# Attention tile ends: who copies four PSUM banks out, where that is emitted, and weight preparation with one more empty step

## The chip, the cores and the metric

The kernel runs on one core of a Trainium2 chip. The metric is device time in microseconds, the median of several runs. Five engines work side by side, each through its own queue in order: TensorE (PE, matmuls; its weight loads are PEld), VectorE (DVE), ScalarE (ACT), GpSimd (POOL) and SyncE (SP), which here only issues DMAs.

## The reference

Attention without softmax, gated by u, and then two feed-forward layers with the same sizes, all in float32:

```python
scores = (1.0 / S) * np.matmul(z, z.transpose(0, 2, 1))      # z: 2 x 3008 x 64
x = u * np.matmul(np.maximum(scores, 0.0) ** 2, v)           # u, v: 2 x 3008 x 256
h = x.reshape(6016, 256) @ w_in1                             # 256 x 2048
x = np.where(h > 0, h, np.exp(np.minimum(h, 0)) - 1) @ w_out1
h = x @ w_in2
out = ((a0 + a1*h + a2*h**2 + a3*h**3) / (1 + abs(b0)*abs(h) + abs(b1)*h**2 + 1e-6)) @ w_out2
```

## The kernel before

Every float32 operand of a matmul is split into a high part and the rest, and a product takes three matmuls: high by high, rest by high, high by rest. Tokens lie along the free axis, so the outputs are transposed (256 features in two halves of 128 partitions, `d` = 0 and 1).

**Attention.** There are 12 query tiles (`spans`, index `ti`): five of 512 tokens and one of 448 for each of two batches. Each is multiplied with 24 chunks of 128 keys (`j`; the last has 64). A step `n` is one tile and chunk, 288 in all (`NA`). At even `n`, `scores(n)` issues six matmuls (L283) for chunks `n` and `n+1` into one of two pairs of banks (0 and 1, or 2 and 3); ScalarE computes the relu (L286) and its square, which is the high part (L287); VectorE multiplies the scores by the relu, in PSUM (L289). At odd `n`, `scores_lo(n-1)` subtracts the high part from that product (L296), which gives the rest and frees the pair of banks. Four steps later (`LAG`), `values(n-4)` multiplies with v: 12 matmuls (L320), each on 64 of the 128 rows, so that two run side by side. They accumulate over the 24 chunks into banks 4 to 7. Key rows 0 to 63 (`h` = 0) and 64 to 127 (`h` = 1) have sums of their own, so `acc[ti][d, h]` are four banks: (1,0) is bank 4, (0,1) bank 5, (0,0) bank 6, (1,1) bank 7. A step's first six matmuls go to banks 4 and 5, the next six to 6 and 7.

**A tile's end** is the `values` of the last chunk, `j` = 23, at step 24 ti + 27. Only banks 6 and 7 still get six matmuls there. `out_of(ti, 1, w)` is emitted ahead of them and empties banks 4 and 5: VectorE multiplies bank 4 by u into `xo` (L339), ScalarE copies bank 5 into `t` (L340). `out_of(ti, 0, w)`, behind them, does the same with 6 and 7 (into `xo` and `e`). GpSimd then multiplies each copy by u (L328) and adds it to `xo` (L329); SP stores `xo` to DRAM (L330). For the last tile VectorE does what GpSimd does for the others. The next tile's first chunk needs banks 4 and 5 right after the six matmuls of the next `scores`.

**Side work.** `todo[n]` holds what else is emitted at step `n`. 32 blocks of the weight matrices arrive as 64-bit words and are turned into float32 pairs in stages: load (SP, L189), four steps later `size` (ScalarE, L197), then one step apart `words` (VectorE, L201 and L203), `powers` (VectorE, L208 and L210), `split` (ScalarE, L216 and L217) and `rest` (three operations on GpSimd, L221 to L228). 18 blocks stay in SBUF (the second batch's steps); 14 are stored to DRAM (L230, L231), during the first batch, and loaded again later. Among these are the loads and splits of v (L160; L169 on ScalarE, L170 on GpSimd), of z (L125; L137 and L138 on VectorE) and the loads of u (L270). Loads of weights, v and u share one tag, `raw`, with three buffers.

**Order.** `manual_schedule` keeps each engine's queue in the order in which the code emits. A step emits `scores` or `scores_lo`, then its `todo`, then `values`, and from step 288 on the steps of the feed-forward layers (`ffn_step`), which take the rest of the time.

Of the kernel before, what the change touches and what calls it, by code (L numbers as in the profile page):

```python
# [11 lines left out]
ALU = mybir.AluOpType  # L12
# [4 lines left out]
def f(ap):  # L17
    return ap.bitcast(F32)
# [3 lines left out]
def attention_then_two_ffns(  # L22
# [16 lines left out]
    nc = tc.nc  # L39
# [16 lines left out]
    for bb in range(B):  # L56
        i0 = 0
        while i0 < S:
            w = min(W, S - i0)
# [26 lines left out]
    def sb(tag, bufs, dt=F32, name=None):  # L86
        return sp.tile([P, W], dt, tag=tag, bufs=bufs, name=name or tag)

    def sb2(tag, bufs, dt=F32R):
        return sp.tile([P, 2, W], dt, tag=tag, bufs=bufs, name=tag)  # L90

    def wide(dt=F32R):
        return wp.tile([P, 2, W], dt, tag="w", name="w")
# [51 lines left out]
    def load_raw():  # L145
        return sp.tile([P, 2, 2 * P, 2], U32, tag="raw", bufs=3, name="raw")
# [31 lines left out]
    def stages_w(which, kind, g, keep):  # L178

        src = ((w_in1, w_out1), (w_in2, w_out2))[which][kind]
        c0 = 2 * g * P
        st = {}

        def load():
            part = src[:, c0:c0 + 2 * P] if kind == 0 else src[c0:c0 + 2 * P]
            raw = load_raw()
            nc.sync.dma_start(  # L189
                out=raw.rearrange("p k f t -> p k (f t)"),  # L190
                in_=part.bitcast(U32).rearrange("(k p) f -> p k f", p=P))
            raw = raw.rearrange("p k f t -> p (k f) t")
            st["lower"], st["upper"] = raw[:, :, 0], raw[:, :, 1]

        def size():
            st["y"] = sb("q", 3, U32)
            nc.scalar.activation(f(st["y"]), f(st["upper"]), AF.Abs)  # L197

        def words():
            y, u = st["y"], st["upper"]  # L200
            nc.vector.scalar_tensor_tensor(  # L201
                out=f(u), in0=f(y), scalar=LEAST, in1=f(u), op0=ALU.is_ge, op1=ALU.mult)
            nc.vector.tensor_scalar(  # L203
                out=y, in0=u, scalar1=3, scalar2=0x3FFFFFFF, op0=ALU.logical_shift_left, op1=ALU.bitwise_and)

        def powers():
            y, u = st["y"], st["upper"]
            nc.vector.scalar_tensor_tensor(  # L208
                out=y, in0=u, scalar=0xC0000000, in1=y, op0=ALU.bitwise_and, op1=ALU.bitwise_or)
            nc.vector.tensor_scalar(out=u, in0=y, scalar1=0xFF800000, scalar2=None, op0=ALU.bitwise_and)  # L210

        def split():
            if keep:
                st["t"] = wide()
            st["hi"] = st["t"][:, 0] if keep else sb("q", 3, F32R)
            nc.scalar.copy(st["hi"], f(st["y"]))  # L216
            nc.scalar.activation(f(st["lower"]), st["lower"], AF.Copy, scale=2.0**-52)  # L217

        def rest():
            hi, y, l = st["hi"], f(st["y"]), f(st["lower"])  # L220
            nc.gpsimd.tensor_tensor(out=y, in0=y, in1=f(hi), op=ALU.subtract)  # L221
            nc.gpsimd.tensor_tensor(out=l, in0=l, in1=f(st["upper"]), op=ALU.mult)
            if keep:
                lo = st["t"][:, 1]
                nc.gpsimd.tensor_tensor(out=lo, in0=y, in1=l, op=ALU.add)
                WS[kind][which, g] = [t.rearrange("p (k f) -> p k f", k=2) for t in (hi, lo)]
            else:
                nc.gpsimd.tensor_tensor(out=y, in0=y, in1=l, op=ALU.add)  # L228
                d = dp.tile([P, 2, W], F32, tag=f"wd{kind}{g}", name=f"wd{kind}{g}")
                nc.sync.dma_start(out=d[:, 0], in_=f(hi))  # L230
                nc.sync.dma_start(out=d[:, 1], in_=y)  # L231
                WD[which, kind, g] = d

        return load, size, words, powers, split, rest

    def stages_reload(which, kind, g):
        st = {}
# [21 lines left out]
    xd = {}  # L259
    hl = {}  # L260
    acc = {}

    us = {}
    LAG = 4
# [7 lines left out]
    def scores(n):  # L272

        ti, j = divmod(n, NCH)
        bb, i0, w = spans[ti]
        r, l = Z[bb, i0 // W]
        sr, sl = Z[bb, j // 4]
        i = n % 4
        s = psum[:, i:i + 2, :w]
        for k, (lhs, rhs) in enumerate(((sr, r), (sl, r), (sr, l))):  # L280
            for h in range(2):
                rows, c = slice(h * DQ, (h + 1) * DQ), (j + h) % 4 * P
                nc.tensor.matmul(s[:, h], lhsT=lhs[rows, c:c + P], rhs=rhs[rows, :w], start=k == 0, stop=k == 2)  # L283
        hi = sb2("hl", 3)
        e = wide(F32)[:, :, :w]
        nc.scalar.activation(e, s, AF.Relu, scale=SCALE)  # L286
        nc.scalar.activation(hi[:, :, :w], e, AF.Square)  # L287

        nc.vector.scalar_tensor_tensor(out=s, in0=s, scalar=SCALE, in1=e, op0=ALU.mult, op1=ALU.mult)  # L289
        hl[n] = hi  # L290

    def scores_lo(n):
        w = spans[n // NCH][2]
        hi, lo = hl.pop(n), sb2("x", 3)
        i = n % 4
        nc.vector.tensor_tensor(  # L296
            out=lo[:, :, :w], in0=psum[:, i:i + 2, :w], in1=f(hi[:, :, :w]), op=ALU.subtract)
        for h in range(2):
            hl[n + h] = hi[:, h], lo[:, h]
        if n >= NA - 4:  # L300
            free_banks.extend((i, i + 1))

    def values(n):
        ti, j = divmod(n, NCH)
        bb, i0, w = spans[ti]
        if j == 0:

            acc[ti] = {way: psum[:, 4 + k] for k, way in enumerate(((1, 0), (0, 1), (0, 0), (1, 1)))}
        hi, lo = hl.pop(n)
        vh, vl = V[bb, j // 2]  # L310
        if j == NCH - 1:
            xd[ti] = dp.tile([P, ND, W], F32, tag=f"xd{ti}", name=f"xd{ti}")
            out_of(ti, 1, w)


        for way in ((1, 0), (0, 1))[j == NCH - 1:]:
            for k, (lhs, rhs) in enumerate(((vh, hi), (vl, hi), (vh, lo))):
                for h, d in enumerate(way):
                    rows = slice(h * P // 2, (h + 1) * P // 2)
                    nc.tensor.matmul(  # L320
                        acc[ti][d, h][:, :w], lhsT=lhs[rows, j % 2, d * P:(d + 1) * P], rhs=rhs[rows, :w],
                        start=j == 0 and k == 0, stop=k == 2 and j == NCH - 1 - (h != d))
        if j == NCH - 1:
            x, y = out_of(ti, 0, w)

            eng = nc.gpsimd if ti < NTL - 1 else nc.vector
            for d in range(ND):
                eng.tensor_tensor(out=y[d], in0=y[d], in1=us[ti][:, d, :w], op=ALU.mult)  # L328
                eng.tensor_tensor(out=x[d], in0=x[d], in1=y[d], op=ALU.add)  # L329
                nc.sync.dma_start(out=xd[ti][:, d, :w], in_=x[d])  # L330
            del acc[ti], us[ti], sums[ti]

    sums = {}

    def out_of(ti, d, w):

        x, y = sums.setdefault(ti, ({}, {}))
        x[d], y[1 - d] = sb("xo", 2)[:, :w], (sb("t", 3) if d else sb("e", 3))[:, :w]
        nc.vector.tensor_tensor(out=x[d], in0=acc[ti][d, 0][:, :w], in1=us[ti][:, d, :w], op=ALU.mult)  # L339
        nc.scalar.copy(y[1 - d], acc[ti][1 - d, 1][:, :w])  # L340
        if ti == NTL - 1:
            free_banks.extend((4, 5) if d else (6, 7))
        return x, y


    a0, a1, a2, a3 = (coef[:, i:i + 1] for i in range(4))
# [18 lines left out]
    def split_x1(ti):  # L365
        w = ftiles[ti][1]
        raw = x1[ti][:, :, :w]
        hi, lo = ([t[:, d, :w] for d in range(ND)] for t in (sb2("rl", 2), sb2("rl", 2)))
        for d in range(ND):
            nc.vector.tensor_copy(hi[d], raw[:, d])  # L370
        for d, eng in enumerate((nc.vector, nc.gpsimd)):
            eng.tensor_tensor(out=lo[d], in0=raw[:, d], in1=f(hi[d]), op=ALU.subtract)
        x1[ti] = list(zip(hi, lo))
# [225 lines left out]
    n = 0  # L599
# [149 lines left out]
    NA = NTL * NCH  # L749
# [26 lines left out]
    for each, n0, n1 in ((halves, 26, HALF - 10), (direct, HALF + 4, NA - 16)):  # L776
        for k, key in enumerate(each):
            n = n0 + k * (n1 - n0) // len(each)
# [8 lines left out]
    for n in sorted(x for x in todo if x < 0):  # L787
        for fn in todo.pop(n):
            fn()
    for n in range(NA + NSTEP):  # L790
        if n < NA and n % 2 == 0:
            scores(n)
        if n < NA and n % 2:
            scores_lo(n - 1)
        for fn in todo.pop(n, ()):
            fn()
        if LAG <= n < NA + LAG:
            values(n - LAG)
        if n == NA - 3:
            split_x1(0)  # L800
        if n >= NA:
            ffn_step(n - NA)
# [30 lines left out]
```

## Time and profile before

| | |
|---|---|
| Time, median of 3 runs | 1642.83 us (1642.64 to 1643.84) |
| The profiled execution | 1645.2 us, of which the span is 1643.4 us |
| PE busy | 1574.1 us, 96% of the span |
| DVE busy | 1396.5 us, 85% |
| ACT busy | 1303.5 us, 79% |
| POOL busy | 746.3 us, 45% |
| Mean granted TensorE clock | 0.985 |

Busy shares are means over stages that differ. A row of the timeline has the start, the duration (of several instructions merged, from the first start to the last end), engine, line, operation and tiles, and in brackets how long the engine had been idle and whose work released it. PEclk is the granted TensorE clock as a share of full speed: 1.00 is 2.4 GHz and 0.50 is 1.2 GHz.

### The profile page before, as it was taken

The page shows a single profiled execution, that of the slowest core. Times are in us where ns is not written, and L with a number is a line of the kernel's source. Part 1 is how long each engine was busy: PE and PEld are TensorE (multiplying, and loading weights), DVE is VectorE, ACT ScalarE, POOL GpSimd, SP SyncE. Part 2 cuts the span into 40 slices and gives each one's busy share as a digit, 9 for nine tenths or more (in the row PEclk, how much of TensorE's full clock was granted, in tenths as well). Part 3 has the DMA queues.
Part 4 walks back from the last instruction along what each step waited for, and adds up shares of the span by engine and source line. Part 5 has one row for each costly group of instructions (what it writes and reads, how often), then busy time and mean ns, then how long its engine had stood idle before and what let it go on. Part 6 is the DMA issues. An engine that isn't in the chain of part 4 may idle for free.

```text
span 1643.4 us, 25037 instructions
## 1 busy us (share of the span) xinstructions
PE 1574.1 (96%) x9240; PEld 1324.9 (81%) x9240; DVE 1396.5 (85%) x1866; ACT 1303.5 (79%) x2035; POOL 746.3 (45%) x591
## 2 busy tenths in 40 slices
PE   8999998999989999999999999999999999998896
PEld 6877897888889888887878787878788787887796
DVE  7787888987877568889898989898888989899998
ACT  6666776776766688988888888889898888887786
POOL 3334443333433354444454444454444445447645
PEclk9999999999999999999999999999999999999999
DMA  4223343112221420000000000000000000000000
GB/s 126 74 92 115 104 134 110 63 59 78 65 65 60 151 66 0 24 1 27 1 1 27 1 26 1 26 1 27 1 27 1 1 20 1 21 0 13 1 14 14
DMA packets 40987, 67.15 MB, mean 41 GB/s; under 512 B 5536, under 2 KB 18336, under 8 KB 40864
## 3 DMA queue, kind: packets, MB, share of 16 engines
q1 hardware_dynamic: 40864, 65.55, 12.5%
q8 instruction: 72, 1.18, 0.3%
q14 instruction: 51, 0.42, 0.1%
HBM read 45.88 MB, written 19.66 MB: 40 GB/s over the span
## 4 chain that ended last, share of the span: by engine, by line
PE 63%; DVE 12%; ACT 5%; issue 3%; POOL 1%; POOLq 0%; DVEq 0%; ACTq 0%
PE psum L320 11%; PE psum L255 8%; PE psum L391 8%; PE psum L392 8%; PE psum L394 8%; PE psum L256 8%; PE psum L254 8%; PE psum L283 3%; DVE x L521 2%; DVE t L523 1%; DVE e L424 1%; DVE q L500 1%; DVE q L522 1%; DVE psum L289 1%; POOL hl L433 1%
## 5 line engine op out<-in xcount | busy, mean ns | idle before, releaser
L527 POOL TENSOR_TENSOR x<-t,r 128x512 fp32r<-128x512 f32 (+1 forms) x182 | 239.7, 1317 | 470.1 <-DVE t L523 455.1
L320 PE MATMUL psum<-hl,w 64*128 64x512 f32 (+1 forms) x2256 | 377.8, 398 | 29.0 <-DVE xo L339 28.0
L320 PEld LDWEIGHTS psum<-hl,w 64*128 64x128 f32 x2256 | 246.7, 190 | 62.2 <-ACT w L286 12.6
L433 POOL TENSOR_TENSOR hl<-e,hl 128x512 fp32r<-128x512 f32 (+1 forms) x192 | 246.2, 1282 | 31.3 <-ACT hl L432 30.2
L320 PE MATMUL psum<-x,w 64*128 64x512 f32 (+1 forms) x1128 | 247.4, 395 | 0.0
L286 ACT ACTIVATE w<-psum 128x1024 f32<-128x1024 f32 (+1 forms) x144 | 145.0, 1007 | 127.8 <-PE psum L283 126.4
L289 DVE SCALAR_TENSOR_TENSOR psum<-psum,w 128x1024 f32<-128x1024 f32 (+1 forms) x144 | 173.9, 1207 | 78.0 <-ACT w L286 77.7
L472 ACT ACTIVATE t<-psum,coef 128x512 f32<-128x512 f32 (+1 forms) x192 | 148.0, 771 | 82.6 <-PE psum L394 82.6
L498 DVE SCALAR_TENSOR_TENSOR q<-q,coef,psum 128x512 f32<-128x512 f32 (+1 forms) x166 | 122.0, 735 | 81.7 <-ACT q L491 81.6
L296 DVE TENSOR_TENSOR x<-psum,hl 128x1024 fp32r<-128x1024 f32 (+1 forms) x144 | 172.9, 1201 | 11.6 <-ACT q L197 0.5
L255 PE MATMUL psum<-hl,w 128*128 128x512 f32 (+2 forms) x416 | 157.4, 378 | 3.1 <-POOL hl L433 2.7
L391 PE MATMUL psum<-x,w 128*128 128x512 f32 (+2 forms) x416 | 154.2, 374 | 5.5 <-DVE t L523 5.5
L391 PE MATMUL psum<-rl,w 128*128 128x512 f32 (+2 forms) x416 | 154.3, 374 | 2.3 <-DVE e L424 1.6
L254 PE MATMUL psum<-hl,w 128*128 128x512 f32 (+2 forms) x416 | 155.8, 374 | 0.5 <-ACT hl L432 0.5
L256 PE MATMUL psum<-hl,w 128*128 128x512 f32 (+2 forms) x416 | 155.6, 374 | 0.0
L287 ACT ACTIVATE hl<-w 128x1024 fp32r<-128x1024 f32 (+1 forms) x144 | 150.5, 1045 | 4.6
L392 PE MATMUL psum<-rl,w 128*128 128x512 f32 (+2 forms) x416 | 153.9, 373 | 0.0
L392 PE MATMUL psum<-x,w 128*128 128x512 f32 (+2 forms) x416 | 153.8, 373 | 0.0
L255 PE MATMUL psum<-x,w 128*128 128x512 f32 (+2 forms) x384 | 147.2, 383 | 3.8 <-POOL x L527 3.7
L254 PE MATMUL psum<-x,w 128*128 128x512 f32 (+2 forms) x384 | 146.7, 382 | 3.1 <-DVE t L523 3.1
L424 DVE SCALAR_TENSOR_TENSOR e<-e,psum 128x512 f32<-128x512 f32 (+1 forms) x192 | 128.5, 669 | 22.3 <-ACT e L419 22.3
L256 PE MATMUL psum<-x,w 128*128 128x512 f32 (+2 forms) x384 | 146.6, 382 | 0.0
(150 smaller groups left out, 3657.5 us busy)
## 6 DMA issues: line engine op xcount, KB each, us to landing
raw<-w_in_dram SPq DMA_DIRECT2D x16, 512.0 KB, 4.1
raw<-w_out_dram SPq DMA_DIRECT2D x16, 512.0 KB, 4.1
wd<-q SPq DMA_DIRECT2D x28, 256.0 KB, 2.3
raw<-wd SPq DMA_DIRECT2D x14, 512.0 KB, 3.5
raw<-v_dram SPq DMA_DIRECT2D x22, 256.0 KB, 3.9
raw<-uT_dram SPq DMA_DIRECT2D x10, 512.0 KB, 4.3
xd<-xo SPq DMA_DIRECT2D x20, 256.0 KB, 2.1
outT_dram<-xo SPq DMA_DIRECT2D x20, 256.0 KB, 2.1
```

The source lines that it names most:

```text
L254: nc.tensor.matmul(out, lhsT=lh, rhs=rh, start=start, stop=False)
L255: nc.tensor.matmul(out, lhsT=lh, rhs=rl, start=False, stop=False)
L256: nc.tensor.matmul(out, lhsT=ll, rhs=rh, start=False, stop=stop)
L287: nc.scalar.activation(hi[:, :, :w], e, AF.Square)
L289: nc.vector.scalar_tensor_tensor(out=s, in0=s, scalar=SCALE, in1=e, op0=ALU.mult, op1=ALU.mult)
L296: nc.vector.tensor_tensor(out=lo[:, :, :w], in0=psum[:, i:i + 2, :w], in1=f(hi[:, :, :w]), op=ALU.subtract)
L320: nc.tensor.matmul(acc[ti][d, h][:, :w], lhsT=lhs[rows, j % 2, d * P:(d + 1) * P], rhs=rhs[rows, :w], start=j == 0 and k == 0, stop=k == 2 ...
L391: nc.tensor.matmul(h[:, cols], lhsT=wh[:, d, c], rhs=x[d][0], start=d == 0, stop=False)
L392: nc.tensor.matmul(h[:, cols], lhsT=wl[:, d, c], rhs=x[d][0], start=False, stop=False)
L433: nc.gpsimd.tensor_tensor(out=lo, in0=e, in1=f(hi), op=ALU.subtract)
L472: act(new("p", "t", 3), h, AF.Identity, bias=a2, scale=a3)
L527: tt(out=st["lo"], in0=st["p"], in1=st["r"], op=ALU.mult)
```

## The change

`out_of` copies both of its banks on ScalarE and no longer multiplies on VectorE. GpSimd (VectorE for the last tile) first adds the two halves of a sum and then multiplies by u, so there are four operations a tile on GpSimd as before. In the main loop `values` is emitted ahead of the step's `todo`; at step 4 alone it comes ahead of `scores` too. An empty stage stands between `powers` and `split`, so `split` and `rest` of every weight block come one step later.

```diff
-        return load, size, words, powers, split, rest
+        return load, size, words, powers, lambda: None, split, rest
...
         if j == NCH - 1:
-            x, y = out_of(ti, 0, w)
+            out_of(ti, 0, w)
 
             eng = nc.gpsimd if ti < NTL - 1 else nc.vector
             for d in range(ND):
-                eng.tensor_tensor(out=y[d], in0=y[d], in1=us[ti][:, d, :w], op=ALU.mult)
-                eng.tensor_tensor(out=x[d], in0=x[d], in1=y[d], op=ALU.add)
-                nc.sync.dma_start(out=xd[ti][:, d, :w], in_=x[d])
+                x, y = sums[ti][d, 0], sums[ti][d, 1]
+                eng.tensor_tensor(out=x, in0=x, in1=y, op=ALU.add)
+                eng.tensor_tensor(out=x, in0=x, in1=us[ti][:, d, :w], op=ALU.mult)
+                nc.sync.dma_start(out=xd[ti][:, d, :w], in_=x)
...
     def out_of(ti, d, w):
 
-        x, y = sums.setdefault(ti, ({}, {}))
-        x[d], y[1 - d] = sb("xo", 2)[:, :w], (sb("t", 3) if d else sb("e", 3))[:, :w]
-        nc.vector.tensor_tensor(out=x[d], in0=acc[ti][d, 0][:, :w], in1=us[ti][:, d, :w], op=ALU.mult)
-        nc.scalar.copy(y[1 - d], acc[ti][1 - d, 1][:, :w])
+        for k, c in enumerate((d, 1 - d)):
+            t = sums.setdefault(ti, {})[c, k] = (sb("xo", 2) if k == 0 else sb("t", 3) if d else sb("e", 3))[:, :w]
+            nc.scalar.copy(t, acc[ti][c, k][:, :w])
         if ti == NTL - 1:
             free_banks.extend((4, 5) if d else (6, 7))
-        return x, y
...
     for n in range(NA + NSTEP):
+
+        if n == LAG:
+            values(0)
         if n < NA and n % 2 == 0:
             scores(n)
         if n < NA and n % 2:
             scores_lo(n - 1)
+        if LAG < n < NA + LAG:
+            values(n - LAG)
         for fn in todo.pop(n, ()):
             fn()
-        if LAG <= n < NA + LAG:
-            values(n - LAG)
```

## Rows read from the trace of the kernel before

**Rows 1.** Windows: length; PE, PEld, DVE, ACT, POOL busy (count); PEclk, DMA share, GB/s.
```profile
0.00:552.00 552.00, 512.10 (x4282) 450.81 (x4283) 447.91 (x475) 377.61 (x445) 207.11 (x171) 0.97 0.28 88
552.00:1643.40 1091.40, 1061.96 (x4960) 874.08 (x4958) 948.57 (x1392) 925.86 (x1590) 539.16 (x420) 0.99 0.05 17
```
**Rows 2.** The waits of PE: total us, times, the longest.
```profile
PE psum L320 <- DVE xo L339: 28.0, 11, 4.5
...
PE psum L320 <- ACT t L340: 1.0, 1, 1.0
```
**Rows 3.** The timeline of PE and ACT at the first tile's end.
```profile
53.51 0.84 PE L283 MATMUL psum<-rl 64*128 64x512 f32 x6
55.98 0.72 PE L320 MATMUL psum<-hl,w 64*128 64x512 f32 x4 [1.63 <-DVE xo L339]
...
58.86 0.87 PE L283 MATMUL psum<-rl 64*128 64x512 f32 x6
...
62.34 0.87 PE L283 MATMUL psum<-rl,x 64*128 64x512 f32 x6
...
52.67 1.06 ACT L287 ACTIVATE hl<-w 128x1024 fp32r<-128x1024 f32 x1
53.64 0.57 ACT L340 COPY t<-psum 128x512 f32<-128x512 f32 x1
54.10 0.59 ACT L340 COPY e<-psum 128x512 f32<-128x512 f32 x1
```
**Rows 4.** The timeline of DVE, ACT and PE at the second tile's end.
```profile
96.96 1.23 DVE L296 TENSOR_TENSOR x<-psum,hl 128x1024 fp32r<-128x1024 f32 x1
98.10 1.49 DVE L201 SCALAR_TENSOR_TENSOR raw<-q,raw 128x512 f32<-128x512 f32 x1
...
99.97 1.28 DVE L339 TENSOR_TENSOR xo<-psum,raw 128x512 f32<-128x512 f32 x2
...
97.14 0.56 ACT L340 COPY t<-psum 128x512 f32<-128x512 f32 x1
...
100.80 1.22 PE L320 MATMUL psum<-hl,w 64*128 64x512 f32 x4 [3.50 <-DVE xo L339]
```
**Rows 5.** The windows: seven stretches after a tile's end, their sum; then two others.
```profile
100.80:106.06 5.26, 5.26 (x24) 4.46 (x26) 4.95 (x5) 1.21 (x2) 4.60 (x4) 0.50 0.15 55
...
508.52:512.60 4.08, 4.08 (x25) 4.08 (x26) 2.55 (x3) 1.25 (x2) 3.92 (x4) 0.58 0.19 68
sum 33.65, PE 33.64 PEld 29.36 DVE 24.88 ACT 6.20 POOL 29.66; mean PE 4.81 PEld 4.19 DVE 3.55 ACT 0.89 POOL 4.24
...
55.98:58.86 2.88, 2.88 (x25) 2.59 (x26) 2.78 (x3) 0.73 (x1) 2.28 (x2) 1.00 0.05 18
235.90:238.41 2.51, 2.51 (x24) 2.45 (x26) 2.41 (x3) 0.68 (x1) 2.43 (x3) 1.00 0.83 261
```
**Rows 6.** The windows around the seventh and the eleventh tile's end.
```profile
322.00:326.00 4.00, 2.38 (x21) 1.80 (x19) 3.90 (x5) 3.97 (x6) 3.12 (x4) 1.00 0.00 0
506.00:510.00 4.00, 2.07 (x16) 1.73 (x15) 3.87 (x5) 3.74 (x6) 3.84 (x4) 0.86 0.00 0
```
**Rows 7.** The timeline of ACT and PE at the ninth tile's end.
```profile
411.14 0.62 ACT L216 CAST w<-q 128x512 fp32r<-128x512 f32 x1 [0.84 <-DVE q L208]
411.67 0.67 ACT L217 ACTIVATE raw<-raw 128x512 f32<-128x512 uint32 x1
...
413.53 0.86 PE L283 MATMUL psum<-x,rl 64*128 64x512 f32 x6
```
**Rows 8.** The timeline of POOL and SP at the third tile's end.
```profile
140.66 1.31 POOL L228 TENSOR_TENSOR q<-q,raw 128x512 f32<-128x512 f32 x1
141.93 1.30 POOL L170 TENSOR_TENSOR w<-raw,w 128x512 fp32r<-128x512 f32 x1
...
143.25 0.38 SPq L160 DMA_DIRECT2D raw<-v_dram  x1
```
**Rows 9.** The page's DMA issues: KB each, median us from issue to landing.
```profile
raw<-v_dram SPq DMA_DIRECT2D x22, 256.0 KB, 3.9
```

## The prediction

> **What bounds the kernel now.** I read the windows by stage first, then PE's waits, then the timeline at tile ends, then the granted clock around them. Attention fills the first 552 us, and there PE is busy 512 of them with ScalarE at 378, VectorE at 448 and GpSimd at 207 [rows 1]: PE sets the pace, and what counts is why it pauses or runs slowly. In PE's waits one line stands out: eleven times, 28.0 us in all, the longest 4.5, a value matmul (L320) waits for VectorE's multiply of bank 4 (L339), and once more, 1.0 us, for a ScalarE copy [rows 2]. These are eleven of the twelve tile ends; the twelfth runs into the feed-forward layers.
>
> At the first one nothing but attention is queued: the scores end at 53.51 + 0.84 = 54.35 and PE goes on at 55.98, 1.63 later; meanwhile ScalarE had copied bank 5 by 54.69 [rows 3]. VectorE is late because L339 stands in its queue behind the subtraction L296, which itself waits for ScalarE. At the second, L296 ends at 98.19, the words of a weight block (1.87 us from 98.10 to 99.97) come next, and L339 starts only at 99.97: PE waits 3.50 [rows 4]. So a long wait is a short one plus weight work.
>
> A second loss follows the wait. After seven of the ends PE runs at a granted clock between 0.50 and 0.65, that is partly or wholly at 1.2 GHz. These seven stretches take 33.65 us; the same work at full clock takes 2.88 us per 24 matmuls of 512, 2.51 for 448 [rows 5], and with 0.70 for six scores matmuls (a fifth of the 3.48 between two scores, [rows 3]) 5 x 2.88 + 3.58 (one stretch holds a scores too) + 2.51 = 20.5. Lost: 13.2. Waits of 1.63 and below left the clock at 1.00 (first and seventh end, [rows 3, 5, 6]); one of 1.93, the eleventh, did not (0.86 in that window, 0.58 after it, [rows 5, 6]). Tile ends thus hold 28.0 + 1.0 + 13.2 = 42.2 us.
>
> **The change, part by part.**
>
> *Copies on ScalarE.* ScalarE reaches a tile's end ahead of L296, since L296 needs its square. At an undisturbed end the copies start 0.13 after the last scores (53.64 against 53.51), 0.46 apart, the second ends 0.59 after its start [rows 3]: banks 4 and 5 are free at 54.69, PE goes on about 0.1 later, 0.45 after 54.35. Six matmuls (0.70) on, at 55.5, it needs bank 7, whose copy is the fourth: 53.64 + 3 x 0.46 + 0.59 = 55.6, with 0.1 a wait of 0.2. That makes 0.65 instead of 1.63. What is late next is ScalarE itself.
>
> *Order at the second, ninth and eleventh ends.* Emitting `values` first takes the same step's weight stage out of the way of the copies, but not a stage of the step before. At the second end `size` is of the step before, copies start at 97.14 as now, so PE goes on at 97.14 + 1.05 + 0.1 = 98.3 against a natural end of 100.80 - 3.50 = 97.3, 1.0, and 0.2 for bank 7. At the ninth and eleventh, `split` moves by its extra step right in front of the copies: 0.53 + 0.57 [rows 7]. Copies at 413.53 + 0.13 + 1.1 = 414.76, PE at 415.9 against 414.39: 1.5, and 0.2; 1.6 for the eleventh. Eight ends at 0.65, then 1.2, 1.7 and 1.6: 9.7 us. The clock should hold at all eleven, the largest single gap being 1.5; the bound is the loss of two stretches, 13.2 / 7 x 2 = 3.8.
>
> *Loads moved past stores.* At the third end the load of v is emitted after the two stores of `xo` instead of before them. It goes out at 143.25 now [rows 8]. Each store waits for two GpSimd operations of 1.3, and in front of these stands the `rest` of a weight block, which ends at 141.97 now [rows 8] and will come behind v's subtraction (1.3) and ScalarE's copy for it (1.0): GpSimd is free about 144.3, the copies are there at 145.4, the stores go at 148.0 and 150.6, the load at 151, landing 3.9 later [rows 9], about 155. ScalarE asks for it some 3 us earlier, and the relu behind it waits as long. From scores to the next use of the same banks PE takes two rounds; the chain there has about 2.1 to spare (rival four). Cost 0.9; bounds 0 and 5.
>
> *Weight stages.* A `split` that moves from an even to an odd step keeps its place among ScalarE's work; one that moves from odd to even goes behind the next relu and square, off their path. Its wait for `powers` (0.84 us at the ninth end, [rows 7]) hid under other work anyway: no gain, no cost. `rest` frees its load buffer a step later. Four loads (steps 46, 71, 96, 121) are emitted in the step in which today's `rest` frees a buffer. I take it that they get the one v's split frees in that same step, so they go out within about 2 us of now.
>
> *Nothing else.* GpSimd does four operations a tile as before, with over half its time idle [rows 1]. VectorE loses 24 multiplies, 1.28 us a tile [rows 4], worth only what is counted above. At the start PE's first value matmuls and third scores wait for the same L296: 0, bounds -0.3 and 0.3. At the last tile two banks pass from VectorE to a ScalarE that also runs the first layer: 0.3, bounds -1 and 1.
>
> Sum: 42.2 - 9.7 - 0.9 - 0.3 = 31.3. The profiled execution took 1645.2 (span 1643.4), so 1613.9 by its own time; it lies 2.4 above the median, and from 1642.8 the forecast is **1611.5 us**.
>
> **The rivals.**
>
> 1. *The loads wait for `rest`* and not for v's split. `rest` is three GpSimd operations, 3.7 us, behind that split, so the load lands about 4 later and `size` holds ScalarE. At the second end the copies stand behind `size`: 3.7 more, and the clock falls again, 2.4 (5.26 against 2.88): 6.1. At the third about 4, at the other two 3.7 less 2.1 to spare: 1.6 each. 13.3 less gain: **1625**. For it: three buffers, all taken. Against: L189's buffer today is free before v's subtraction at 141.93 is done [rows 8], so a load takes what is free first.
>
> 2. *The clock falls after short gaps too.* Then eleven ends each lose 13.2 / 7 = 1.9, 21 in all: gain 31.3 - 21, **1632**. The rows speak against it: 1.63 of wait, clock 1.00 [rows 3, 5]. The Trainium skill (TensorE: Matmul & The Clock Gate, "A second HAM failure mode: psum-queue depth-cycling") says that short idles between groups of matmuls which cycle through banks can make the clock swing between its levels. By that rule this rival would hold; this trace, with 1.00 after 1.63, agrees only for longer waits.
>
> 3. *The gain is eaten, near 1642*: the wait passes from banks 4 and 5 to the scores. Speaks for it that VectorE is at 81% in attention; against, that it loses work.
>
> 4. *Slower.* The four copies put the next relu 0.93 later than two do. At the first end it starts at 55.5, its chain (relu and square 1.05 each, two VectorE operations of 1.23 to 1.33) ends near 59.2, and PE needs the bank pair back at 55.0 + 2 x 2.78 + 0.70 = 61.3: 2.1 to spare, 0.4 to 0.8 where `words` and `powers` fall in between. PE then waits at the scores instead. It decides against the change once the chain is late by 42.2 / 11 + 2.1 = 6 us at a typical end; with 0.5 beyond that at each, **1648**.
>
> 5. *Copies hide fully*: 31.3 + 9.7, **1602**.
>
> **How the numbers follow.** Forecast 0.70, its own range 1606 to 1618; rival one 0.12, two 0.06, three 0.03, four 0.04, five 0.05. The range 1604 to 1627 leaves out two, three, four and part of five, some 0.16. 0.2% of 1643 is 3.3 us, about what a measurement tells from no change: faster 0.93, same 0.03, slower 0.04.
>
> **What would show it.** L339 gone from PE's waits; PE waiting at L320 for ScalarE's copies, about 0.5 at eight ends, 1.0 to 1.5 at three, some 10 us in all; granted clock 1.00 through attention; attention's end near 521 instead of 552 and the rest as long as before; near the third end ScalarE waiting for a load of v. Wrong would be: waits of PE at L283 for VectorE growing beyond their present few us, the clock still near 0.5 after tile ends, `size` waiting for its load, or a gain outside attention.

## The result, and the profile after

The changed kernel takes **1624.61 us** (median of 4 runs, 1622.82 to 1626.97) against 1643.26 us for the kernel before (4 runs, 1642.64 to 1643.84): a ratio of 0.9887, 95% interval 0.987 to 0.9905. It is faster by 18.65 us; 31.3 were forecast. The profiled execution took 1626.97 us (span 1625.0, mean granted clock 0.991).

The windows by stage of the changed kernel, in the columns of [rows 1], come first. The second stretch is as long as before (1092.3 us, 1091.4 then), so the 19.3 us by which the stage's end moves all lie in attention: PE's busy time there is the same (512.89 and 512.10), and what shrank is its pauses.

```profile
0.00:532.70 532.70, 512.89 (x4282) 430.84 (x4283) 435.86 (x449) 388.69 (x469) 210.92 (x171) 0.99 0.29 91
532.70:1625.00 1092.30, 1064.20 (x4960) 876.71 (x4958) 948.85 (x1394) 926.06 (x1590) 539.08 (x420) 0.99 0.05 17
```

In PE's waits after (total, times, longest), L339 is gone, as it had to be; of the 29.0 us in [rows 2], 3.4 are left. But the waits at the scores (L283) have grown from 6.1 us to 9.9 and now stand at the top. The first line is of the kernel before, the others are of the changed one.

```profile
PE psum L283 <- DVE x L296: 6.1, 4, 3.0
...
PE psum L283 <- DVE x L296: 9.9, 8, 4.0
...
PE psum L320 <- ACT xo L340: 3.4, 4, 1.0
```

The first tile end after, timeline of PE and ACT; it answers to [rows 3]. The copies start 0.13 after the scores, PE goes on with bank 4 at 55.07, and no idle is noted before it. The four matmuls that took 0.63 a moment earlier take 1.21, since bank 5 comes free only at 55.50. From these scores to the next it is 58.50 - 54.32 = 4.18 us; undisturbed it is 3.48, so the end costs 0.70, and it cost 1.87 before (58.86 - 53.51 - 3.48).

```profile
54.32 0.85 PE L283 MATMUL psum<-rl 64*128 64x512 f32 x6
55.07 1.21 PE L320 MATMUL psum<-hl,w 64*128 64x512 f32 x4
...
58.50 1.07 PE L283 MATMUL psum<-rl 64*128 64x512 f32 x6
...
54.45 0.57 ACT L340 COPY xo<-psum 128x512 f32<-128x512 f32 x1
54.91 0.59 ACT L340 COPY t<-psum 128x512 f32<-128x512 f32 x1
```

The second end after, timeline of ACT and PE, answers to [rows 4]. A `size` of the step before (L197) stands in front of the copies and has waited 0.45 for its load; PE waits 1.02 instead of 3.50.

```profile
96.98 0.66 ACT L197 ACTIVATE q<-raw 128x512 f32<-128x512 f32 x1 [0.45 <-DMA raw<-w_in_dram]
97.55 0.57 ACT L340 COPY xo<-psum 128x512 f32<-128x512 f32 x1
...
98.17 1.22 PE L320 MATMUL psum<-hl,w 64*128 64x512 f32 x4 [1.02 <-ACT xo L340]
```

The ninth end after, same view, answers to [rows 7]: `split` (L216, L217) now stands right in front of the copies, and PE waits 0.98.

```profile
402.40 0.67 ACT L217 ACTIVATE raw<-raw 128x512 f32<-128x512 uint32 x1
402.96 0.57 ACT L340 COPY xo<-psum 128x512 f32<-128x512 f32 x1
...
403.59 1.20 PE L320 MATMUL psum<-hl,w 64*128 64x512 f32 x4 [0.98 <-ACT xo L340]
```

Windows after, in the columns of [rows 5, 6]. From PE's first value matmul after the first and the second tile end to the next scores it is 3.43 us each, at a clock of 1.00; at the second end, 24 matmuls alone took 5.26 before. From 126 to 248 the clock is 1.00 throughout, as it is up to 110 and from 256 on. The two stretches at about half speed follow other pauses.

```profile
55.07:58.50 3.43, 3.43 (x27) 2.46 (x26) 2.04 (x2) 3.40 (x5) 2.36 (x2) 1.00 0.02 5
98.17:101.60 3.43, 3.43 (x24) 2.41 (x26) 1.95 (x3) 3.40 (x5) 2.36 (x2) 1.00 0.26 77
122.40:126.00 3.60, 3.56 (x18) 2.82 (x20) 3.46 (x5) 2.91 (x5) 1.16 (x1) 0.54 0.20 75
...
252.00:256.00 4.00, 4.00 (x28) 3.63 (x26) 3.85 (x6) 3.52 (x5) 3.03 (x3) 0.57 0.18 68
126.00:248.00 122.00, 119.94 (x1018) 98.05 (x1014) 98.90 (x99) 90.71 (x111) 57.97 (x47) 1.00 0.37 118
```

**Where the rest went.** I took the start of every scores (L283) from PE's timeline in both traces and compared the time from one to the next. Over the eleven tile ends these times add up to 82.58 us before and 50.34 after: 32.24 won. From first to last scores only 19.43 is won. The other 12.81 is lost at places that are no tile ends:

| from scores ... | before | after | lost |
|---|---|---|---|
| 62 to 66 | 6.95 | 12.02 | 5.07 |
| 132 to 138 | 12.58 | 15.48 | 2.90 |
| 274 to 276 | 3.09 | 4.24 | 1.15 |
| 224 to 226 | 3.48 | 4.17 | 0.69 |
| 78 to 80 | 4.11 | 4.68 | 0.57 |
| 0 to 6 (start) | 11.14 | 11.62 | 0.48 |

Smaller differences make up the rest. The largest is read from the timeline of SP, POOL, ACT, PE and DVE after, 105 to 123 us. From the end backwards: scores 64 (122.44) wait 3.04 for L296; VectorE had idled 5.66 for the relu of scores 60; that relu (117.92) stands behind a `size` (117.36) that idled 5.54 for its load. The releaser is given as the load from w_in, which landed last. In the order of the code this `size` belongs to the load from w_out (L189 at 111.85), which landed 5.4 later, at 117.28. That load could not leave earlier: ahead of it in SP's queue is the store L231, which left at 111.49, when GpSimd had finished `rest` (110.15 + 1.31 = 111.46).

```profile
111.49 0.32 SPq L231 DMA_DIRECT2D wd<-q  x1
111.85 0.43 SPq L189 DMA_DIRECT2D raw<-w_out_dram  x1
112.79 0.38 SPq L160 DMA_DIRECT2D raw<-v_dram  x1
113.27 0.42 SPq L189 DMA_DIRECT2D raw<-w_in_dram  x1
...
106.51 1.31 POOL L170 TENSOR_TENSOR w<-raw,w 128x512 fp32r<-128x512 f32 x1 [1.53 <-ACT w L169]
...
110.15 1.31 POOL L228 TENSOR_TENSOR q<-q,raw 128x512 f32<-128x512 f32 x1
...
117.36 0.66 ACT L197 ACTIVATE q<-raw 128x512 f32<-128x512 f32 x1 [5.54 <-DMA raw<-w_in_dram]
117.92 1.02 ACT L286 ACTIVATE w<-psum 128x1024 f32<-128x1024 f32 x1
...
122.44 1.45 PE L283 MATMUL psum<-x,t 64*128 64x512 f32 x6 [3.04 <-DVE x L296]
...
118.97 1.23 DVE L289 SCALAR_TENSOR_TENSOR psum<-psum,w 128x1024 f32<-128x1024 f32 x1 [5.66 <-ACT w L286]
120.11 0.68 DVE L201 SCALAR_TENSOR_TENSOR raw<-q,raw 128x512 f32<-128x512 f32 x1
120.82 0.43 DVE L203 TENSOR_SCALAR q<-raw 128x512 uint32<-128x512 uint32 x1
```

Over the whole execution these waits of `size` grew from 7.5 us in four (before: 5.0 for w_out, 2.5 for w_in) to the 15.1 below for w_in and 1.5 more for w_out. It is ACT's line in the view of the waits after:

```profile
ACT q L197 <- DMA raw<-w_in_dram: 15.1, 7, 5.5
```

### The profile page after: what moved, and what is told of

It reads as the page before. It is cut to its first block, busy times and chain, and to the rows that moved or that the text cites. A ratio compares the mean times of both kernels' runs of the same rounds, so it can differ in the third digit from the quotient of the medians.

```text
span 1625.0 us, 25025 instructions
## 1 busy us (share of the span) xinstructions
PE 1577.1 (97%) x9240; PEld 1307.5 (80%) x9240; DVE 1384.7 (85%) x1842; ACT 1314.8 (81%) x2059; POOL 750.0 (46%) x591
## 3 DMA queue, kind: packets, MB, share of 16 engines
q1 hardware_dynamic: 40864, 65.55, 12.6%
## 4 chain that ended last, share of the span: by engine, by line
PE 66%; DVE 10%; ACT 5%; issue 3%; POOL 1%; POOLq 0%; DVEq 0%; ACTq 0%
PE psum L320 11%; PE psum L255 9%; PE psum L390 9%; PE psum L256 9%; PE psum L391 9%; PE psum L393 9%; PE psum L254 8%; PE psum L283 3%; DVE x L520 1%; DVE t L522 1%; DVE e L423 1%; DVE q L499 1%; DVE e L521 1%; ACT e L418 1%; DVE q L521 1%
## 5 line engine op out<-in xcount | busy, mean ns | idle before, releaser
L320 PE MATMUL psum<-hl,w 64*128 64x512 f32 (+1 forms) x2256 | 394.9, 394 | 4.5 <-ACT xo L340 3.4
L320 PEld LDWEIGHTS psum<-hl,w 64*128 64x128 f32 x2256 | 275.5, 187 | 49.7 <-ACT xo L340 7.6
L320 PE MATMUL psum<-x,w 64*128 64x512 f32 (+1 forms) x1128 | 289.4, 390 | 0.5 <-DVE x L296 0.5
L296 DVE TENSOR_TENSOR x<-psum,hl 128x1024 fp32r<-128x1024 f32 (+1 forms) x144 | 172.9, 1200 | 11.3
L320 PEld LDWEIGHTS psum<-x,w 64*128 64x128 f32 x1128 | 164.7, 186 | 19.3 <-DVE x L296 1.2
L390 PE MATMUL psum<-x,w 128*128 128x512 f32 (+2 forms) x416 | 155.2, 377 | 5.0 <-DVE t L522 5.0
L391 PE MATMUL psum<-x,w 128*128 128x512 f32 (+2 forms) x416 | 154.8, 376 | 0.0
L255 PE MATMUL psum<-x,w 128*128 128x512 f32 (+2 forms) x384 | 147.7, 385 | 3.8 <-POOL x L526 3.7
L254 PE MATMUL psum<-x,w 128*128 128x512 f32 (+2 forms) x384 | 147.1, 383 | 3.2 <-DVE t L522 3.1
```

What stands on the lines that cost most here:

```text
L254: nc.tensor.matmul(out, lhsT=lh, rhs=rh, start=start, stop=False)
L255: nc.tensor.matmul(out, lhsT=lh, rhs=rl, start=False, stop=False)
L296: nc.vector.tensor_tensor(out=lo[:, :, :w], in0=psum[:, i:i + 2, :w], in1=f(hi[:, :, :w]), op=ALU.subtract)
L320: nc.tensor.matmul(acc[ti][d, h][:, :w], lhsT=lhs[rows, j % 2, d * P:(d + 1) * P], rhs=rhs[rows, :w], start=j == 0 and k == 0, stop=k == 2 ...
L390: nc.tensor.matmul(h[:, cols], lhsT=wh[:, d, c], rhs=x[d][0], start=d == 0, stop=False)
L391: nc.tensor.matmul(h[:, cols], lhsT=wl[:, d, c], rhs=x[d][0], start=False, stop=False)
```

## The experiments

Theory: the tile ends gave what was forecast, and the empty stage cost about a third of it, because `rest` ends later, its stores leave later, and the load behind them in SP's queue comes too late for its `size`. Rivals: the new order of the loop did it (`values` ahead of loads), or the load buffer that `rest` frees a step later.

**Without the empty stage** (from the changed kernel):

```diff
-        return load, size, words, powers, lambda: None, split, rest
+        return load, size, words, powers, split, rest
```

> The changed kernel without the empty stage between powers and split. Theory (the SP queue): split and rest a step later put the two stores of a stored weight block in front of loads that today leave before them, and ScalarE's size then waits for its load. Then the 5.1 us lost around scores 62 and 64 and about 3 of the loss around scores 132 go, and the ninth and eleventh tile ends, where split stands right in front of the copies, lose about 1 us less each: 1614 to 1617 us. Rival A (ScalarE itself is too full with four copies a tile end): the same losses stay, 1622 to 1626. Rival B (the load waits for its buffer until rest is done): as the theory here, 1614 to 1617; the run with later stores tells these two apart.

1615.65 us (1614.42 to 1615.89; before on the same chip 1644.55): ratio 0.9824, interval 0.981 to 0.9839, clear of the changed kernel's. The empty stage costs about 9 us (9.0 by the medians, 10.4 by the two ratios to the kernel before). From scores 62 to 66 takes 6.96 as in the kernel before. SP and ACT at that place, with the columns of the timeline:

```profile
106.99 0.32 SPq L231 DMA_DIRECT2D wd<-q  x1
107.35 0.43 SPq L189 DMA_DIRECT2D raw<-w_out_dram  x1
...
111.81 0.67 ACT L197 ACTIVATE q<-raw 128x512 f32<-128x512 f32 x1 [1.77 <-DMA raw<-v_dram]
```

Here scores 60 start at 110.42, so the load leaves 3.07 ahead of them; with the empty stage it was 112.09 - 111.85 = 0.24 ahead. 2.83 later, and landing in 5.4 instead of 4.4: that is 3.8, and the wait of `size` grew from 1.77 to 5.54, by 3.77. Without the empty stage nobody waits for this `size`. The second, ninth and eleventh ends are shorter too, by 0.5 each (4.99, 4.97 and 4.56 from scores to scores, against 5.51, 5.45 and 5.02); 1 was expected at each of the last two. Of the 3 expected at scores 132, 1.9 go.

**`todo` ahead of `values` again**, with the empty stage and the copies:

```diff
-        if n == LAG:
-            values(0)
...
-        if LAG < n < NA + LAG:
-            values(n - LAG)
         for fn in todo.pop(n, ()):
             fn()
+        if LAG <= n < NA + LAG:
+            values(n - LAG)
```

> The changed kernel with the step's side work emitted ahead of values again, as before; the empty stage and the copies on ScalarE stay. Theory: the stalls of late loads stay, since the empty stage makes them; at the third tile end size stands in front of the copies again and may wait for its load there: 1 to 3 us more; the start gets back 0.6: 1624 to 1628 us. If the order is what made loads late (stores of xo in front of them): faster, 1618 to 1622. If the order is what cured the long waits: over 1632.

1625.03 us (1623.11 to 1626.58), ratio 0.9882 (0.9868 to 0.9897): no different from the changed kernel. From scores 62 to 66 it still takes 9.82, with the loads emitted where they were before. Of the 5.07 lost there 2.87 stay, so the empty stage costs time without the new order too; the other 2.20 appear only with both, and the totals don't show them.

**The copies alone** (kernel before, with the changed `out_of` and GpSimd's adds and multiplies, nothing else):

```diff
-        nc.vector.tensor_tensor(out=x[d], in0=acc[ti][d, 0][:, :w], in1=us[ti][:, d, :w], op=ALU.mult)
-        nc.scalar.copy(y[1 - d], acc[ti][1 - d, 1][:, :w])
+        for k, c in enumerate((d, 1 - d)):
+            t = sums.setdefault(ti, {})[c, k] = (sb("xo", 2) if k == 0 else sb("t", 3) if d else sb("e", 3))[:, :w]
+            nc.scalar.copy(t, acc[ti][c, k][:, :w])
```

> The kernel before with the copies of all four banks on ScalarE and GpSimd's add and multiply alone; neither the order of emission nor the empty stage is changed. Theory: the copies alone carry the gain at the tile ends (about 31 us, less 2 at the third end, where size stands in front of them), and no load is later than before: 1613 to 1618 us. Rival A (ScalarE too full): no better than the whole change, 1622 to 1628. If all three parts are needed: 1630 to 1640.

1619.97 us (1618.77 to 1620.32), ratio 0.9851 (0.9836 to 0.9865). That is 2 us above the range expected by the theory. Even so one edit of three gives 24.6 us, more than all three together. Against the run with the empty stage and the same order it is 5.1 us less: the empty stage costs in either order. What the new order adds is visible at the third end. There `size`, emitted ahead of the copies in the same step, waits for its load, and the copies and PE wait with it (ACT and PE):

```profile
142.24 0.66 ACT L197 ACTIVATE q<-raw 128x512 f32<-128x512 f32 x1 [2.90 <-DMA raw<-w_out_dram]
...
143.42 1.21 PE L320 MATMUL psum<-hl,w 64*128 64x512 f32 x4 [3.48 <-ACT xo L340]
```

From these scores to the next it is 9.21 us, and 4.18 with the new order: a loss of 5.0 at this end, where 2 were expected.

**Only the stores later** (from the changed kernel, `rest` where it was; its two stores in a stage of their own, one step later):

```diff
-                nc.sync.dma_start(out=d[:, 0], in_=f(hi))
-                nc.sync.dma_start(out=d[:, 1], in_=y)
+                st["d"] = d
...
+        def put():
+            if not keep:
+                nc.sync.dma_start(out=st["d"][:, 0], in_=f(st["hi"]))
+                nc.sync.dma_start(out=st["d"][:, 1], in_=f(st["y"]))
...
-        return load, size, words, powers, lambda: None, split, rest
+        return load, size, words, powers, lambda: None, split, rest, put
```

> The changed kernel with the two stores of a stored weight block in a stage of their own, one step behind rest, so that a load emitted in the step of rest goes ahead of them in SP's queue. Theory (the SP queue): the load for scores 62 leaves some 6 us earlier, the 5.1 us lost there go, about 2 of those at scores 132 may stay (that load stands behind the stores of xo): 1617 to 1621 us. Rival B (the buffer is held until rest is done): no change, 1623 to 1626. Rival A (ScalarE too full): no change, 1623 to 1626.

1621.8 us (1620.93 to 1622.86), ratio 0.9865 (0.9849 to 0.9882). The total lies between the two expected ranges and hardly tells it from the changed kernel, but the place does: from scores 62 to 66 takes 6.96 again. SP and ACT (this kernel's lines 235 and 236 are the two stores; the second waits for `rest`):

```profile
104.08 0.42 SPq L189 DMA_DIRECT2D raw<-w_out_dram  x1
...
110.16 0.32 SPq L236 DMA_DIRECT2D wd<-q  x1
...
110.38 0.64 ACT L197 ACTIVATE q<-raw 128x512 f32<-128x512 f32 x1
```

The load leaves before `rest` has run, so its buffer was free all along, and `size` doesn't wait. The rival of the buffers falls at this place, and the queue is shown. What it wins there it partly loses at scores 132, where the time to the next scores is 9.10 instead of 7.29: the stores now hold a tile of tag `q` longer, ACT waits 2.00 for it (`DMA wd<-q`), and another `size` waits 3.84 for its load.

**The new order alone** (kernel before with the changed main loop; the reverse of the second experiment's diff):

> The kernel before with values emitted ahead of the step's side work and nothing else; VectorE still multiplies two of the banks. Theory (the copies carry the gain): only the side work of the same step leaves VectorE's queue in front of L339, so the wait falls from 3.50 to about 1.6 at the second end and by about 1.1 at the eighth and tenth, while the z split of the sixth and the words of the eighth and tenth stay; most of the slow stretches at the lower clock stay too: a gain of 7 to 13 us, 1631 to 1637. If the order is worth as much as the copies: 1618 to 1626.

1634.6 us (1633.69 to 1635.23; before on the same chip 1644.2), ratio 0.9939 (0.9927 to 0.9952), inside what was expected. DVE and PE at its second end, where L339 now comes ahead of the words:

```profile
97.52 1.23 DVE L296 TENSOR_TENSOR x<-psum,hl 128x1024 fp32r<-128x1024 f32 x1
98.66 1.28 DVE L339 TENSOR_TENSOR xo<-psum,raw 128x512 f32<-128x512 f32 x2
...
99.49 0.72 PE L320 MATMUL psum<-hl,w 64*128 64x512 f32 x4 [1.62 <-DVE xo L339]
```

The 3.50 of [rows 4] become 1.62, which is the short wait of [rows 3]. Copies alone (24.6) and order alone (9.6) add up to 34.2; both together, the first experiment, give 28.9. They overlap by 5.3. By the traces the second end alone shows 4.3 of it: 9.62 from scores to scores before, 4.96 with the copies, 5.37 with the order, 4.99 with both, since either of them takes the words out of the way.

**Loads first** (first experiment, but a step's loads go ahead of `values`, its other stages behind; the start as before):

```diff
+        fns = todo.pop(n, ())
+        for fn in fns:
+            if fn.__name__ == "load":
+                fn()
         if LAG <= n < NA + LAG:
             values(n - LAG)
-        for fn in todo.pop(n, ()):
-            fn()
+        for fn in fns:
+            if fn.__name__ != "load":
+                fn()
```

> The changed kernel without the empty stage, with a step's loads emitted ahead of values (in front of the stores of xo) and its other side work behind, and with the first values behind the third scores as before. Theory (the SP queue): the v load near the third end leaves ahead of the stores of xo and the 1.4 us lost at scores 78 go; the start gets 0.6 back: 2 us less than without the empty stage alone, 1612 to 1615. Rival (that loss is ScalarE's four copies and size, not the load): no change, 1615 to 1617.

1616.01 us (1614.85 to 1616.4), ratio 0.9825 (0.9812 to 0.9838): the same as without it. The load of v at the third end left ahead of the stores of `xo`, and from scores 78 to 80 it still takes 4.68. So that load was never what cost there.

**The z-split of the second batch on GpSimd as well** (added to the one before):

```diff
-            nc.vector.tensor_tensor(out=l, in0=zr, in1=f(r), op=ALU.subtract)
+            (nc.gpsimd if bb else nc.vector).tensor_tensor(out=l, in0=zr, in1=f(r), op=ALU.subtract)
```

> The run with loads first, and with the subtraction of the second batch's z splits on GpSimd instead of VectorE. Around scores 132 to 136 all versions lose 3 to 4 us. Theory: VectorE is the bound there, with z splits, words and powers in one stretch, so 0.7 us less for each of three z splits gives 1 to 2.5 us: 1610 to 1614. Rival (late loads hold size there): no change, within 1 us of the run with loads first.

1615.11 us (1614.2 to 1616.69), ratio 0.9823 (0.9809 to 0.9836). The difference of 0.9 us is inside both ranges; from scores 132 to 134 it takes 5.13, against 5.12. VectorE's z-split is not shown to cost anything there.

The last two and the first experiment can't be told apart; the simplest of them, the changed kernel without its empty stage, beats the kernel before by 28.9 us and the changed one by about 9.

## Why the prediction was right, and where not

**The time: in the range, partly by luck.** 1624.61 lies between 1604 and 1627, but 6.6 above the forecast's own range of 1606 to 1618. The wider range holds it because it takes in rival one, whose mechanism is not what happened. The mechanism of the copies was right; the rest of the gap is mainly the empty stage.

**The copies: right.** 42.2 less 9.7, 32.5 us, were forecast for the eleven ends, and 32.24 measured. That the two agree so closely is luck: with 3.48 as the natural time from scores to scores (3.08 at the fifth and the eleventh end, where the next tile has 448 columns) the ends cost 45.1 before and 12.9 after, both some 3 above the forecast, and the errors cancel. Of the 12.9, 2.2 go with the empty stage. At the first the end costs 0.70 (forecast 0.65). The second is the one that was most under-sized: 5.51 - 3.48 = 2.0, forecast 1.2; 0.5 of it goes with the empty stage (4.99 without), where `size` has waited 0.45 for its load. The ninth and eleventh came out at 5.45 - 3.48 = 2.0 and 5.02 - 3.08 = 1.9 (forecast 1.7 and 1.6). Most of these residues don't appear as waits: only 3.4 of the forecast 10 us stand in PE's waits, because PE goes on with bank 4 and its matmuls stretch.

**The clock: right.** It stayed at 1.00 after each tile end, so rival two falls. The longest wait left there is 1.02. The rule of the Trainium skill that was weighed for that rival (TensorE: Matmul & The Clock Gate, "A second HAM failure mode: psum-queue depth-cycling") doesn't show at such pauses here. The clock did fall after the pauses of 3.04 and 3.96 at the scores.

**Loads moved past stores: the reason wrong, the size near by luck.** The load of v at the third end left at 152.12 (forecast 151), in time for ScalarE's cast at 154.87, since it landed in 2.7. From scores 78 to 80 1.20 is lost (forecast 0.9), 0.57 more than before. The timeline of DVE and PE there shows another cause:

```profile
147.97 1.23 DVE L289 SCALAR_TENSOR_TENSOR psum<-psum,w 128x1024 f32<-128x1024 f32 x1 [1.94 <-ACT w L286]
149.11 1.41 DVE L201 SCALAR_TENSOR_TENSOR raw<-q,raw 128x512 f32<-128x512 f32 x1
150.55 1.42 DVE L203 TENSOR_SCALAR q<-raw 128x512 uint32<-128x512 uint32 x1
151.89 1.21 DVE L296 TENSOR_TENSOR x<-psum,hl 128x1024 fp32r<-128x1024 f32 x1
...
153.16 0.98 PE L283 MATMUL psum<-x,x 64*128 64x512 f32 x6 [0.80 <-DVE x L296]
```

The relu comes late, behind four copies and `size`, and then the words (2.8 us) stand in front of L296. It is rival four on a small scale: the chain late by more than its slack, at one end of eleven.

**Weight stages: wrong, and this is the step that failed.** "no gain, no cost" was said of the stage that moves, and "they go out within about 2 us of now" of four loads. The prediction asked whether a buffer would be free, at the steps where `rest` frees one. It did not follow the two stores that `rest` issues: they are in SP's queue too, the second waits for GpSimd, and every load emitted later waits behind it, whatever its buffer. At scores 62 the end of `rest` came 2.8 later than without the empty stage: `split` (104.75) now went behind a relu and square, and on GpSimd v's subtraction (L170 at 106.51) came first. Said to cost nothing, the empty stage cost about 9 us (5.1 with `todo` first). By the two traces 5.07 of it is at scores 62 to 66, some 1.9 at 132 to 138, 0.5 at each of the second, ninth and eleventh ends, 0.7 at the fifth, 0.7 and 1.15 at scores 224 and 274; that is 11 between two profiled executions which lie 12.6 apart, more than their medians. The Trainium skill (DMA: Bandwidth & Descriptors, "Anatomy of one DMA — SWDGE (gpsimd) path"), in a section on DMAs that GpSimd issues, says that a wait on a semaphore happens on the sequencer that issues the DMA, ahead of dispatch. The trace agrees, here for SP: the store left 0.03 after GpSimd's end, and the load 0.36 after the store.

The stores are not the whole of it. With the stores later, the second, ninth and eleventh ends (5.42, 5.34, 5.05) and scores 224 and 274 (4.16 and 4.24) stay as long as in the changed kernel; the second batch, where the last four lie, stores no weights. Around scores 274 the traces show another path: a step later, `rest` runs on GpSimd while VectorE does `words` and `powers` of other blocks, and L203 and L210 take about 1.0 us longer each. That makes L296, for which scores 276 wait, 2.0 later, of which 1.15 reach PE. VectorE and GpSimd there, the changed kernel first, then without the empty stage:

```profile
495.76 1.41 DVE L203 TENSOR_SCALAR q<-raw 128x512 uint32<-128x512 uint32 x1
498.81 1.43 DVE L210 TENSOR_SCALAR raw<-q 128x512 uint32<-128x512 uint32 x1
...
495.12 1.77 POOL L221 TENSOR_TENSOR q<-q,w 128x512 f32<-128x512 f32 x1
...
484.32 0.43 DVE L203 TENSOR_SCALAR q<-raw 128x512 uint32<-128x512 uint32 x1
...
486.38 0.43 DVE L210 TENSOR_SCALAR raw<-q 128x512 uint32<-128x512 uint32 x1
...
487.23 1.30 POOL L221 TENSOR_TENSOR q<-q,w 128x512 f32<-128x512 f32 x1 [3.50 <-ACT w L216]
```

At scores 224 L210 takes 1.15 beside `rest` and 0.43 without it, which is the 0.7 there.

**Rival one** named 1625, and that is nearly the time; its mechanism was another. It had the loads wait for a buffer, costing 6.1 at the second end and 4 at the third; measured there is 0.5 and nothing, and at scores 62 the buffer was free. At the second end the load did wait for a buffer, the one that v's split frees, as the prediction supposed: it left at 92.58, 0.03 after GpSimd's subtraction for v (91.25 + 1.30). Rival three falls with the 32.24, rival five with the 12.9 that the ends still cost; four holds only as said above.

**The start: forecast 0, lost 0.5.** `values(0)` ahead of the third scores makes the step from scores 2 to 4 longer by 1.60 and the next shorter by 1.12. That the order costs the 0.5 is not shown: from scores 0 to 6 the first experiment takes 10.56 with the same start, and the one with loads first 12.11 with the start as before.

**Open.** From scores 132 to 138 even the kernel before loses 12.58 - 3 x 3.08 = 3.3 us (3.08 is the natural time with 448 columns). The changed kernel's SP, ACT and PE show two stores of `xo` waiting for GpSimd in front of a load, and a `size` waiting for that load:

```profile
236.73 3.29 SPq L331 DMA_DIRECT2D xd<-xo  x2
240.07 0.43 SPq L189 DMA_DIRECT2D raw<-w_in_dram  x1
...
245.78 0.67 ACT L197 ACTIVATE q<-raw 128x512 f32<-128x512 f32 x1 [2.94 <-DMA raw<-w_in_dram]
...
251.57 0.88 PE L283 MATMUL psum<-r,x 64*128 64x448 f32 x6 [3.96 <-DVE x L296]
```

That is the same pattern, but no experiment removed it: 4.3 us over the natural time are left without the empty stage, 4.1 with the loads first, and 4.3 with the z-split moved. Why the fifth end is 0.7 shorter both without the empty stage and with the stores later was not followed. A fourth load buffer was not tried.

## What to carry to other kernels

When a stage of side work moves by a step, follow every DMA that it issues in its queue: a store that waits for a slow engine holds back all loads behind it, and the price shows up steps later as a wait for a load in an engine that stands ahead of the critical chain. Test the parts of a change one by one: here the part that looked free took back a third of the gain, and the change without it was the best version. A moved copy pays twice when the wait that it shortens had been long enough for the clock to fall.

## What the runs showed of the hardware

- **Loads that leave together land later.** Three loads that left SP within 1.4 us (111.85 to 113.27) landed after 5.2 to 6.0 us; over the page of the changed kernel the medians are 4.3 (512 KB) and 3.0 (256 KB).
- **Some of VectorE's words and powers took two to three times as long beside GpSimd.** With GpSimd idle, L201 and L203 took 0.68 and 0.43 us (120.11, 120.82); while GpSimd added and multiplied a tile's sums (148.67 to 151.67) they took 1.41 and 1.42. No run took GpSimd away there. At scores 274 one did: without the empty stage L203 and L210 took 0.43 each instead of 1.41 and 1.43; L201 and L208 took 0.68 either way.
- **The clock after a pause of PE**: 1.00 after 1.02, 0.54 behind 3.04 and 0.57 behind 3.96. That goes with the kernel before: 1.00 after 1.63 and 0.50 after 3.50 [rows 3 to 5].
